# A decode block on one core: w_gate loaded first, its product and GELU ahead of q, the constants ahead of the statistics

## The chip, the core and the metric

The kernel runs on one core of a Trainium2 chip. The metric is the device time of one execution in microseconds (us). One execution was also recorded by the hardware profiler; its rows are what this document reads.

## The reference

One decode step for eight tokens. x (8 × 512) is normalised; attention over the last 1024 positions of a k and a v cache (32 query heads, 8 key heads, 128 wide) gives s; a GELU-gated feed-forward (512 to 1792 to 512) of the same normalised x gives g.

```
xn = layernorm(x)
q = xn @ wq                                   # 8 x 4096
s = softmax(q k^T / sqrt(128)) v @ wo         # window: last 1024 of 4096 positions
g = silu((gelu(xn @ w_gate) * (xn @ w_up)) @ w_down)
out = x + s * g
```

All tensors are bf16. The core reads 47.46 MB: 32 MiB of caches, 4 MiB each of wq and wo, and 1.75 MiB each of w_gate, w_up and w_down.

## The kernel before

The order of work on every engine is the program order; the kernel schedules it by hand. All large loads are issued by SP into one DMA queue, in this order: wq, k of batches 0 and 1, v of batch 0, then in the batch loop k of batch b+2 and v of batch b+1, and after the loop w_gate, w_up, w_down and wo. Each k or v of a batch is two loads of 1 MiB. x goes in five small pieces through ScalarE's queue (L78).

SBUF has eight slots of 16 KB per partition. `slot` (L66) hands them out in turn; two of the eight lie where wq lies, so the first loads that take these two (k of batch 3, v of batch 2) wait until the q product is done. A load into a used slot waits for the last reader of what lay there. Each DMA also waits for the eighth one before it, whose semaphore it takes over.

The front: VectorE (DVE) writes a few constants, waits for x, computes mean and variance (L137, L139), ScalarE the root (L141), and x normalised is transposed by TensorE (PE) into xnR (L159 to L161). Then the q product (L254) fills eight PSUM banks with 32 matmuls. Behind the statistics DVE and GpSimd (POOL) write the masks and selectors (neg_st, neg_mv, sel, own, pick, oT) and DVE clears qbd (L245), a block-diagonal copy of q. q is cast to bf16, transposed and copied into qbd (L264 to L277).

The loop: for each batch `turn_k` (L242) transposes k on DVE, `scores` (L304) multiplies it by qbd, `softmax` (L312) takes maximum and exponent, `turn_p` (L337) transposes the weights, `values` (L348) multiplies by v, and `gather` and `regroup` (L369 to L400) put the heads where the wo product wants them.

The tail: products of xnR with w_gate (z_ps) and w_up (u_ps) at L459, GELU of z by the tanh form (L469 to L477), the product with u (L479), a transpose (L482), the product with w_down (f_ps, L488), silu (L496 to L500), the product with wo (s_ps, L507) in four parts as wo lands, two DVE steps (L515, L517) and the store (L519).

Of the kernel before, what the change touches and what calls it, by code (L numbers as in the profile page):

```python
# [7 lines left out]
ACT = mybir.ActivationFunctionType  # L8
ALU = mybir.AluOpType
AX = mybir.AxisListType  # L10
BF16 = mybir.dt.bfloat16
FP32 = mybir.dt.float32
I32 = mybir.dt.int32
PSUM = bass.MemoryType.PSUM

N_SLOTS = 8
RB = 4
# [4 lines left out]
def kernel(  # L22
# [13 lines left out]
    nc = tc.nc  # L36

    B, Sq, D = A_x.shape
    Hkv, Sk, Dh = A_k_cache.shape[1], A_k_cache.shape[2], A_k_cache.shape[3]
    Hq = A_wq.shape[1] // Dh  # L40
# [3 lines left out]
    F = B_w_gate.shape[1]  # L44
    inv = float(Dh) ** -0.5
    P = nc.NUM_PARTITIONS
    NK = D // P
    HG = 4
    NG = Hkv // HG
    C = W * HG // P  # L50
    ROW = C * Dh
    FT = F // 4
    NJ = F // P
    DT = D // 4
# [3 lines left out]
    keep = ctx.enter_context(tc.tile_pool(name="keep", bufs=1))  # L58
# [7 lines left out]
    def slot(name):  # L66
        i = taken[0] % N_SLOTS
        taken[0] += 1
        if i >= 2:
            return ring.tile([P, 2 * ROW], BF16, name=name, tag="slot")  # L70
        if not late:
            late.append(ctx.enter_context(tc.tile_pool(name="late", bufs=2)))
        return late[0].tile([P, 2 * ROW], BF16, name=name, tag="slot")


    x_sb = keep.tile([B, D], BF16, name="x_sb")
# [19 lines left out]
    def load_v(b):  # L96
        v_sb[b] = load_cache(A_v_cache, b, "v_sb")

    wq_v = A_wq.rearrange("(p k) n -> p k n", k=NK)
    wq_all = wq_pool.tile([P, NK, Hq * Dh], BF16, name="wq_sb")  # L100
    nc.sync.dma_start(out=wq_all, in_=wq_v)
    wq_sb = [wq_all[:, k, :] for k in range(NK)]
# [5 lines left out]
    ident = consts.tile([P, P], BF16, name="ident")  # L108
    nc.vector.memset(ident, 0.0)
    nc.gpsimd.affine_select(  # L110
        out=ident,
        in_=ident,
# [6 lines left out]
    eps_sb = consts.tile([B, 1], FP32, name="eps_sb")  # L119
    nc.vector.memset(eps_sb, 1e-5)  # L120
    xnR = keep.tile([P, NK, 4, 32], BF16, name="xnR")
    nc.vector.memset(xnR, 0.0)
    xpad = keep.tile([B, 32], BF16, name="xpad")
    nc.gpsimd.memset(xpad, 0.0)
    nc.gpsimd.affine_select(
        out=xpad,
        in_=xpad,
# [3 lines left out]
        pattern=[[-1, 32]],  # L131
        channel_multiplier=RB,
    )


    stats = keep.tile([B, nc.vector.BN_STATS_DIM], FP32, name="stats")
    nc.vector.bn_stats(out=stats, in_=x_sb)  # L137
    mv = keep.tile([B, nc.vector.BN_AGGR_DIM], FP32, name="mv")
    nc.vector.bn_aggr(out=mv, in_=stats)  # L139
    rstd = keep.tile([B, 1], FP32, name="rstd")  # L140
    nc.scalar.activation(out=rstd, in_=mv[:, 1:2], func=ACT.Sqrt, bias=eps_sb, scale=1.0)  # L141
    nc.vector.reciprocal(out=rstd, in_=rstd)
    xhat = keep.tile([B, D], BF16, name="xhat")
    nc.vector.tensor_scalar(  # L144
        out=xhat,
        in0=x_sb,
        scalar1=mv[:, 0:1],
        scalar2=rstd[:, 0:1],
        op0=ALU.subtract,
        op1=ALU.mult,  # L150
    )
    x_res = keep.tile([P, DT], FP32, name="x_res")
    warm = keep.tile([B, 1], FP32, name="warm")
    nc.scalar.activation(out=warm, in_=rstd, func=ACT.Exp)  # L154
    with tc.tile_pool(name="ps_x", bufs=1, space=PSUM) as ps_x:
        xnT_ps = ps_x.tile([P, NK, B], BF16, name="xnT_ps")
        xv = xhat.rearrange("b (p k) -> b k p", k=NK)
        for k in range(NK):
            nc.tensor.transpose(xnT_ps[:, k, :], xv[:, k, :], ident[0:B, 0:B])  # L159
        for j in range(4):  # L160
            nc.vector.tensor_copy(out=xnR[:, :, j, 0 : RB * B : RB], in_=xnT_ps)  # L161
        xr_ps = ps_x.tile([P, DT], FP32, name="xr_ps")
        for t in range(4):
            nc.tensor.matmul(
                xr_ps[32 * t : 32 * t + 32, :],
                xpad,
                x_sb[:, t * DT : (t + 1) * DT],
                start=True,
                stop=True,
            )  # L170
        nc.scalar.copy(out=x_res, in_=xr_ps)  # L171

    qd = Hq // NG
# [6 lines left out]
        out=hv,  # L182
        in_=hv,
# [7 lines left out]
        out=neg_st,  # L191
        in_=neg_st,
# [8 lines left out]
        out=neg_mv,  # L201
        in_=neg_mv,
# [5 lines left out]
    )  # L208

    NU = Hq // 8
    sel = consts.tile([P, NG, Hq], FP32, name="sel")
    nc.vector.memset(sel, 0.0)
    for g in range(NG):
        nc.vector.tensor_reduce(
            out=sel[:, g, g * qd : (g + 1) * qd],
            in_=ident.rearrange("p (t g h) -> p g h t", t=4, g=NG)[:, g],
            axis=AX.X,
            op=ALU.add,  # L220
# [3 lines left out]
        out=own, in_=ident.rearrange("p (i e) -> p e i", e=8), axis=AX.X, op=ALU.add  # L224
    )
    pick = consts.tile([P, 4 * NU], BF16, name="pick")
    with nc.allow_low_precision(reason="sums of zeros and a single one"):
        nc.vector.tensor_reduce(
            out=pick, in_=ident.rearrange("p (a e) -> p a e", e=8), axis=AX.X, op=ALU.add
# [2 lines left out]
    nc.vector.memset(oT, 0.0)  # L232

    qbd = keep.tile([P, 2, B, 2, NG, 4 * Hq], BF16, name="qbd")
    kT = {}

    def turn_k(b, g):  # L240
        t = kT_pool.tile([P, ROW], BF16, name="kT")
        nc.vector.transpose(out=t.bitcast(I32), in_=k_sb[b][:, g].bitcast(I32))  # L242
        kT[b, g] = t

    nc.vector.memset(qbd, 0.0)  # L245
    turn_k(0, 0)
    q_both = slot("q_both")
    q_bf = q_both[:, 0:ROW]
# [1 line left out]
    with tc.tile_pool(name="ps_q", bufs=1, space=PSUM) as ps_q:  # L250
        q_ps = [ps_q.tile([P, 512], FP32, name=f"q_ps{i}") for i in range(8)]
        for k in range(NK):
            for i in range(8):
# [4 lines left out]
                    start=(k == 0),  # L258
                    stop=(k == NK - 1),
# [165 lines left out]
            regroup(0)  # L425


    wgu = []
    for w in (B_w_gate, B_w_up):
        tv = slot("wgu_sb")[:, 0 : NK * F].rearrange("p (k f) -> p k f", k=NK)  # L430
        nc.sync.dma_start(out=tv, in_=w.rearrange("(p k) f -> p k f", k=NK))
        wgu.append(tv)
    wd = slot("wd_sb")[:, 0 : NJ * D].rearrange("p (j d) -> p j d", d=D)
    nc.sync.dma_start(out=wd, in_=B_w_down.rearrange("(p j) d -> p j d", j=NJ))
    wo = []
    for u in range(NU):
        if u % 2 == 0:
            pair = slot("wo_sb").rearrange("p (v j d) -> p v j d", v=2, d=D)
        t = pair[:, u % 2]
# [11 lines left out]

    ps_f = ctx.enter_context(tc.tile_pool(name="ps_f", bufs=1, space=PSUM))
    ffn = ctx.enter_context(tc.tile_pool(name="ffn", bufs=1))
    zu = []
    for n, ws in (("z_ps", wgu[0]), ("u_ps", wgu[1])):
        ps = ps_f.tile([P, FT], FP32, name=n)
        for k in range(NK):
            for t in range(4):
                nc.tensor.matmul(  # L459
                    ps[32 * t : 32 * t + 32, :],  # L460
                    xnR[:, k, t, :],
                    ws[:, k, t * FT : (t + 1) * FT],
                    start=(k == 0),
                    stop=(k == NK - 1),
                )
        zu.append(ps)
    z_ps, u_ps = zu
    z2 = ffn.tile([P, FT], FP32, name="z2")
    nc.scalar.activation(out=z2, in_=z_ps, func=ACT.Square)  # L469
    nc.vector.tensor_scalar(  # L470
        out=z2, in0=z2, scalar1=0.044715, scalar2=1.0, op0=ALU.mult, op1=ALU.add
    )
    nc.vector.tensor_tensor(out=z2, in0=z2, in1=z_ps, op=ALU.mult)
    th = ffn.tile([P, FT], FP32, name="th")
    nc.scalar.activation(out=th, in_=z2, func=ACT.Tanh, scale=0.7978845608028654)
    nc.vector.tensor_scalar(out=th, in0=th, scalar1=0.5, scalar2=0.5, op0=ALU.mult, op1=ALU.add)
    nc.vector.tensor_tensor(out=th, in0=th, in1=z_ps, op=ALU.mult)  # L477
    h_bf = ffn.tile([P, FT], BF16, name="h_bf")
    nc.vector.tensor_tensor(out=h_bf, in0=th, in1=u_ps, op=ALU.mult)  # L479

    hT = ffn.tile([P, NJ, 32], BF16, name="hT")
    nc.vector.transpose(  # L482
        out=hT.rearrange("p j b -> p (j b)"), in_=h_bf.rearrange("p (y j) -> p j y", j=NJ)
    )
    f_ps = ps_f.tile([P, DT], FP32, name="f_ps")
    for j in range(NJ):
        for t in range(4):
# [4 lines left out]
                start=(j == 0),  # L492
                stop=(j == NJ - 1),
# [4 lines left out]
        out=g_sb, in0=g_sb, scalar1=0.5, scalar2=0.5, op0=ALU.mult, op1=ALU.add  # L498
# [5 lines left out]
    for u in range(NU):  # L504
        for j in range(8):
            for t in range(4):
# [4 lines left out]
                    start=(u == 0 and j == 0),  # L511
                    stop=(u == NU - 1 and j == 7),
# [7 lines left out]
        out=out_f.rearrange("b (t d) -> t b d", t=4), in_=out_sb[0 : P : RB, :]  # L520
# [31 lines left out]
```

## Time and profile before

| | |
|---|---|
| median of 3 runs (lowest to highest) | 121.13 us (120.96 to 121.29) |
| the profiled execution | 121.08 us |
| its span | 119.2 us |
| busy: PE, DVE, ACT, POOL | 70.9, 75.7, 31.4, 3.2 us |
| mean rate of the DMA engines | 399 GB/s |
| share of DMA in the chain that ended last | 78% |

The span runs from the first instruction to the last; 1.86 us of the profiled execution lie around it. In the rows of slices a digit is the busy share of a fortieth of the span, in tenths. In the chain that ended last each piece is what released the next. In a timeline a row has its start in us, its duration, the engine, the line, the operation and its tiles; in a list of waits the numbers are the total in us, how often, and the longest. SPq is SP's instruction queue, in which a load's issue stands until its waits are met.

### The profile page before, as it was taken

Reading aid. Unit: us, or ns where it says so; the run is one execution under the profiler, and the core shown is the slowest. Engines: PE = TensorE matmul, PEld = TensorE weight load, DVE = VectorE, ACT = ScalarE, POOL = GpSimd, SP = SyncE. Lnnn points to the kernel's source line nnn. Section 1 sums busy time; section 2 is a strip of 40 time slices with the busy share of each in tenths; the row PEclk is TensorE's granted clock in tenths of the full one; section 3 lists DMA queues with packets and bytes.
Section 4 is the critical chain, followed back from the end, with each engine's and each line's share of the span. In section 5 each row is a group of like instructions: output and inputs, shape, how many; then the busy total and the mean of one; then the engine's idle time right before and its main releaser. Section 6 shows DMA issues by size and latency. Waiting matters only on the chain.

```text
span 119.2 us, 2306 instructions
## 1 busy us (share of the span) xinstructions
PE 70.9 (59%) x992; PEld 37.9 (32%) x992; DVE 75.7 (63%) x101; ACT 31.4 (26%) x75; POOL 3.2 (3%) x10
## 2 busy tenths in 40 slices
PE   0000079971299498896969692875783547544370
PEld 0000033420034154453635451433452433143350
DVE  1000387969998999999999968949952241751000
ACT  0300240076500715144161700421618101100000
POOL 2000052000000000000000000000000000000000
PEclk9999999998559999999999999999999755555555
DMA  6898899999999999999999999999999999999930
GB/s 177 352 518 363 374 429 432 423 429 426 434 418 423 434 426 421 426 432 418 423 432 426 421 423 429 423 429 421 423 429 433 443 438 404 438 414 429 402 140 3
DMA packets 6110, 47.61 MB, mean 399 GB/s; under 512 B 716, under 2 KB 852, under 8 KB 1108
## 3 DMA queue, kind: packets, MB, share of 16 engines
q1 hardware_dynamic: 6084, 47.46, 94.7%
q8 instruction: 8, 0.13, 0.4%
q14 instruction: 2, 0.02, 0.0%
q10 hardware_dynamic: 16, 0.01, 0.0%
HBM read 47.46 MB, written 0.01 MB: 398 GB/s over the span
## 4 chain that ended last, share of the span: by engine, by line
DMA 78%; PE 9%; DVE 6%; ACT 2%; issue 1%; ACTq 1%; DVEq 0%; SPq 0%
DMA k_sb<-in_A_k_cache_dram 32%; DMA wo_sb<-in_A_wo_dram 20%; DMA v_sb<-in_A_v_cache_dram 16%; DMA x_sb<-in_A_x_dram 9%; PE q_ps L254 8%; DVE qbd L277 3%; ACTq L78 1%; DVE q_both L267 1%; ACT L154 1%; DVE q_both L264 1%; PE s_ps L507 1%; DVE stats L137 1%; DVE y L515 0%; ACT rstd L141 0%; DVE out_sb L517 0%
## 5 line engine op out<-in xcount | busy, mean ns | idle before, releaser
L304 PE MATMUL S_ps<-kT,qbd 128*128 128x512 bf16 x128 | 31.9, 393 | 14.8 <-DVE kT L242 11.3
L242 DVE STREAM_TRANSPOSE kT<-k_sb 128x2048 int32<-128x2048 int32 x16 | 36.5, 2286 | 1.6 <-DMA k_sb<-in_A_k_cache_dram 1.6
L304 PEld LDWEIGHTS <-qbd 128*128 128x128 bf16 x128 | 12.6, 99 | 30.8 <-issue 14.2
L324 ACT ACTIVATE nb<-m 32x1 f32<-32x1 f32 x32 | 6.4, 201 | 20.1 <-DVE m L321 19.8
L326 ACT ACTIVATE P_sb<-S_ps,nb 128x1024 bf16<-128x1024 f32 x8 | 11.1, 1390 | 0.3
L348 PE MATMUL O_ps<-v_sb,pT 128*32 128x128 bf16 x512 | 9.2, 227 | 2.6 <-DVE pT L337 2.6
L314 DVE TENSOR_REDUCE mx<-S_ps 128x1 f32<-128x1024 f32 x8 | 9.6, 1194 | 1.6 <-PE S_ps L304 1.6
L254 PE MATMUL q_ps<-wq_sb,xnR 128*128 128x512 bf16 x32 | 9.9, 485 | 0.5 <-ACT x_res L171 0.5
L348 PEld LDWEIGHTS <-pT 128*32 128x32 bf16 x512 | 7.7, 100 | 5.6 <-issue 3.0
L159 PE MATMUL xnT_ps<-ident,xhat 8*128 8x8 bf16 x4 | 0.3, 174 | 15.2 <-DVE xhat L144 15.2
L361 ACT COPY O_sb<-O_ps 128x256 f32<-128x256 f32 x8 | 3.0, 372 | 22.7 <-PE O_ps L348 22.7
L137 DVE BATCH_NORM_STATS2 stats<-x_sb 8x6 f32<-8x512 bf16 x1 | 0.7, 681 | 12.0 <-DMA x_sb<-in_A_x_dram 12.0
L337 DVE STREAM_TRANSPOSE pT<-P_sb 128x512 int32<-128x512 int32 x8 | 5.7, 711 | 3.4 <-ACT P_sb L326 3.3
L507 PE MATMUL s_ps<-wo_sb,oT 128*32 128x128 bf16 x128 | 4.4, 307 | 3.9 <-DMA wo_sb<-in_A_wo_dram 3.9
L369 PE MATMUL o_ps<-O_sb,sel 128*32 128x128 f32 x32 | 5.4, 297 | 0.9 <-ACT O_sb L361 0.9
L293 PE MATMUL S_ps<-neg_mv,neg_st 128*128 128x512 bf16 x16 | 4.8, 381 | 1.9 <-DVE q_both L264 1.9
L254 PEld LDWEIGHTS <-xnR 128*128 128x128 bf16 x32 | 3.8, 118 | 6.4 <-issue 3.9
L264 ACT CAST q_both<-q_ps 128x512 bf16<-128x512 f32 x6 | 3.0, 613 | 8.6 <-PE q_ps L254 8.6
L507 PEld LDWEIGHTS <-oT 128*32 128x32 bf16 x128 | 3.5, 136 | 4.9 <-issue 4.7
L159 PEld LDWEIGHTS <-xhat 8*128 8x128 bf16 x4 | 0.2, 113 | 15.2 <-DVE xhat L144 15.2
L515 DVE TENSOR_TENSOR y<-s_ps,g_sb 128x128 f32<-128x128 f32 x1 | 0.3, 292 | 7.4 <-PE s_ps L507 7.4
L369 PEld LDWEIGHTS o_ps<-O_sb,sel 128*32 128x32 f32 x32 | 3.0, 115 | 4.0 <-issue 2.5
(64 smaller groups left out, 53.9 us busy)
## 6 DMA issues: line engine op xcount, KB each, us to landing
k_sb<-in_A_k_cache_dram SPq DMA_DIRECT2D x16, 1024.0 KB, 16.5
v_sb<-in_A_v_cache_dram SPq DMA_DIRECT2D x16, 1024.0 KB, 19.8
wq_sb<-in_A_wq_dram SPq DMA_DIRECT2D x1, 4096.0 KB, 12.2
wo_sb<-in_A_wo_dram SPq DMA_DIRECT2D x3, 1024.0 KB, 25.0
wgu_sb<-in_B_w_gate_dram SPq DMA_DIRECT2D x1, 1792.0 KB, 21.3
wgu_sb<-in_B_w_up_dram SPq DMA_DIRECT2D x1, 1792.0 KB
wd_sb<-in_B_w_down_dram SPq DMA_DIRECT2D x1, 1792.0 KB
wo_sb<-in_A_wo_dram SPq DMA_DIRECT2D x1, 640.0 KB
```

What stands on the lines that cost most here:

```text
L242: nc.vector.transpose(out=t.bitcast(I32), in_=k_sb[b][:, g].bitcast(I32))
L254: nc.tensor.matmul(q_ps[i], xnR[:, k, :, :].rearrange("p j b -> p (j b)"), wq_sb[k][:, i * 512 : (i + 1) * 512], start=(k == 0), stop=(k = ...
L264: e(out=q_bf[:, i * 512 : (i + 1) * 512], in_=q_ps[i])
L293: nc.tensor.matmul(S[b][:, half, :], neg_st.rearrange("p j h -> p (j h)"), neg_mv.rearrange("p a n -> p (a n)"), start=True, stop=False,)
L304: nc.tensor.matmul(S[b][:, half, :], qbd[:, m, b, w, g, :], kv[:, half * 16 : (half + 1) * 16, m, :, w], start=False, stop=(g == NG - 1 an ...
L314: nc.vector.tensor_reduce(out=mx, in_=S[b].rearrange("p a c -> p (a c)"), axis=AX.X, op=ALU.max)
L324: nc.scalar.mul(nb[32 * j : 32 * j + 32, :], m1, -inv)
L326: nc.scalar.activation(out=P_sb[b].rearrange("p c i w -> p c w i"), in_=S[b].rearrange("p a (c w i) -> p (a c) w i", w=2, i=32), func=ACT.Exp,
L337: nc.vector.transpose(out=pT[b].rearrange("p c h w -> p (c h w)").bitcast(I32), in_=P_sb[b].rearrange("p c i w -> p (c i w)").bitcast(I32),)
L348: nc.tensor.matmul(O_ps[b][32 * t : 32 * t + 32, g, :], pT[b][:, c // 2, :, c % 2], vv[:, c, :], start=(c < 4), stop=(c >= C - 4),)
L369: nc.tensor.matmul(o[:, 0:Dh], sel[:, g, :], O_sb[b][:, g, :], start=(g == 0), stop=(g == NG - 1))
L507: nc.tensor.matmul(s_ps[32 * t : 32 * t + 32, :], oT[:, j, u, :], wo[u][:, j, t * DT : (t + 1) * DT], start=(u == 0 and j == 0), stop=(u = ...
```

## The change

w_gate becomes the first load of SP's queue, ahead of wq. Its slot is the first of the eight, so the slots of later tiles move on by one: v of batch 1 and k of batch 3 now take the two that lie on wq. The masks and selectors, and the clearing of qbd, move ahead of x's statistics on DVE and POOL. The product with w_gate is placed ahead of the q product on PE, in a PSUM pool of its own (`ps_z`) that is closed before q's pool opens, and the GELU is placed ahead of the first `turn_k` on DVE and ahead of q's casts on ScalarE; its result is kept in a new tile, gz. After the loop only w_up is loaded and multiplied, and h_bf is gz times u_ps. The arithmetic is the same.

```diff
+    def load_ffn(w):
+        t = slot("wgu_sb")[:, 0 : NK * F].rearrange("p (k f) -> p k f", k=NK)
+        nc.sync.dma_start(out=t, in_=w.rearrange("(p k) f -> p k f", k=NK))
+        return t
+
+    wg_sb = load_ffn(B_w_gate)
     wq_all = wq_pool.tile([P, NK, Hq * Dh], BF16, name="wq_sb")
     nc.sync.dma_start(out=wq_all, in_=wq_v)
...
+    (neg_st, neg_mv, sel, own, pick, oT and the clearing of qbd, unchanged, from below)
     stats = keep.tile([B, nc.vector.BN_STATS_DIM], FP32, name="stats")
     nc.vector.bn_stats(out=stats, in_=x_sb)
...
+    gz = keep.tile([P, 512], FP32, name="gz")[:, 0:FT]
...
+    def project(ps, ws):
+        for k in range(NK):
+            for t in range(4):
+                nc.tensor.matmul(ps[32 * t : 32 * t + 32, :], xnR[:, k, t, :],
+                    ws[:, k, t * FT : (t + 1) * FT], start=(k == 0), stop=(k == NK - 1))
+
+    zctx = ExitStack()
+    ps_z = zctx.enter_context(tc.tile_pool(name="ps_z", bufs=1, space=PSUM))
+    z_ps = ps_z.tile([P, FT], FP32, name="z_ps")
+    project(z_ps, wg_sb)
...
-    nc.vector.memset(qbd, 0.0)
+    with tc.tile_pool(name="gelu", bufs=1) as gelu:
+        (the six GELU steps, unchanged, from below; the last writes gz)
+    zctx.close()
     turn_k(0, 0)
...
-    wgu = []
-    for w in (B_w_gate, B_w_up):
-        ...
+    wu_sb = load_ffn(B_w_up)
...
-    zu = []
-    for n, ws in (("z_ps", wgu[0]), ("u_ps", wgu[1])):
-        ...
-    (the six GELU steps)
+    u_ps = ps_f.tile([P, FT], FP32, name="u_ps")
+    project(u_ps, wu_sb)
     h_bf = ffn.tile([P, FT], BF16, name="h_bf")
-    nc.vector.tensor_tensor(out=h_bf, in0=th, in1=u_ps, op=ALU.mult)
+    nc.vector.tensor_tensor(out=h_bf, in0=gz, in1=u_ps, op=ALU.mult)
```

More of the change, by code (lines that the diff above doesn't have):

```diff
@@ L133 @@
     )
[L136 to L171, printed above, removed]
     qd = Hq // NG
@@ L237 @@
     qbd = keep.tile([P, 2, B, 2, NG, 4 * Hq], BF16, name="qbd")
+    nc.vector.memset(qbd, 0.0)
+    stats = keep.tile([B, nc.vector.BN_STATS_DIM], FP32, name="stats")
+    nc.vector.bn_stats(out=stats, in_=x_sb)
+    mv = keep.tile([B, nc.vector.BN_AGGR_DIM], FP32, name="mv")
+    nc.vector.bn_aggr(out=mv, in_=stats)
+    rstd = keep.tile([B, 1], FP32, name="rstd")
+    nc.scalar.activation(out=rstd, in_=mv[:, 1:2], func=ACT.Sqrt, bias=eps_sb, scale=1.0)
+    nc.vector.reciprocal(out=rstd, in_=rstd)
+    xhat = keep.tile([B, D], BF16, name="xhat")
+    nc.vector.tensor_scalar(
+        out=xhat,
+        in0=x_sb,
+        scalar1=mv[:, 0:1],
+        scalar2=rstd[:, 0:1],
+        op0=ALU.subtract,
+        op1=ALU.mult,
+    )
+    x_res = keep.tile([P, DT], FP32, name="x_res")
+    gz = keep.tile([P, 512], FP32, name="gz")[:, 0:FT]
+    warm = keep.tile([B, 1], FP32, name="warm")
+    nc.scalar.activation(out=warm, in_=rstd, func=ACT.Exp)
+    with tc.tile_pool(name="ps_x", bufs=1, space=PSUM) as ps_x:
+        xnT_ps = ps_x.tile([P, NK, B], BF16, name="xnT_ps")
+        xv = xhat.rearrange("b (p k) -> b k p", k=NK)
+        for k in range(NK):
+            nc.tensor.transpose(xnT_ps[:, k, :], xv[:, k, :], ident[0:B, 0:B])
+        for j in range(4):
+            nc.vector.tensor_copy(out=xnR[:, :, j, 0 : RB * B : RB], in_=xnT_ps)
+        xr_ps = ps_x.tile([P, DT], FP32, name="xr_ps")
+        for t in range(4):
+            nc.tensor.matmul(
+                xr_ps[32 * t : 32 * t + 32, :],
+                xpad,
+                x_sb[:, t * DT : (t + 1) * DT],
+                start=True,
+                stop=True,
+            )
+        nc.scalar.copy(out=x_res, in_=xr_ps)
+    def project(ps, ws):
+        for k in range(NK):
+            for t in range(4):
+                nc.tensor.matmul(
+                    ps[32 * t : 32 * t + 32, :],
+                    xnR[:, k, t, :],
+                    ws[:, k, t * FT : (t + 1) * FT],
+                    start=(k == 0),
+                    stop=(k == NK - 1),
+                )
+    zctx = ExitStack()
+    ps_z = zctx.enter_context(tc.tile_pool(name="ps_z", bufs=1, space=PSUM))
+    z_ps = ps_z.tile([P, FT], FP32, name="z_ps")
+    project(z_ps, wg_sb)
     kT = {}
@@ L243, in turn_k @@
         kT[b, g] = t
-    nc.vector.memset(qbd, 0.0)
+    with tc.tile_pool(name="gelu", bufs=1) as gelu:
+        z2 = gelu.tile([P, FT], FP32, name="z2")
+        nc.scalar.activation(out=z2, in_=z_ps, func=ACT.Square)
+        nc.vector.tensor_scalar(
+            out=z2, in0=z2, scalar1=0.044715, scalar2=1.0, op0=ALU.mult, op1=ALU.add
+        )
+        nc.vector.tensor_tensor(out=z2, in0=z2, in1=z_ps, op=ALU.mult)
+        th = gelu.tile([P, FT], FP32, name="th")
+        nc.scalar.activation(out=th, in_=z2, func=ACT.Tanh, scale=0.7978845608028654)
+        nc.vector.tensor_scalar(
+            out=th, in0=th, scalar1=0.5, scalar2=0.5, op0=ALU.mult, op1=ALU.add
+        )
+        nc.vector.tensor_tensor(out=gz, in0=th, in1=z_ps, op=ALU.mult)
+    zctx.close()
     turn_k(0, 0)
@@ L425 @@
             regroup(0)
-    wgu = []
-    for w in (B_w_gate, B_w_up):
-        tv = slot("wgu_sb")[:, 0 : NK * F].rearrange("p (k f) -> p k f", k=NK)
-        nc.sync.dma_start(out=tv, in_=w.rearrange("(p k) f -> p k f", k=NK))
-        wgu.append(tv)
+    wu_sb = load_ffn(B_w_up)
     wd = slot("wd_sb")[:, 0 : NJ * D].rearrange("p (j d) -> p j d", d=D)
@@ L453 @@
     ffn = ctx.enter_context(tc.tile_pool(name="ffn", bufs=1))
-    zu = []
-    for n, ws in (("z_ps", wgu[0]), ("u_ps", wgu[1])):
[L456 to L477, printed above, removed]
+    u_ps = ps_f.tile([P, FT], FP32, name="u_ps")
+    project(u_ps, wu_sb)
     h_bf = ffn.tile([P, FT], BF16, name="h_bf")
-    nc.vector.tensor_tensor(out=h_bf, in0=th, in1=u_ps, op=ALU.mult)
+    nc.vector.tensor_tensor(out=h_bf, in0=gz, in1=u_ps, op=ALU.mult)
     hT = ffn.tile([P, NJ, 32], BF16, name="hT")
```

## The prediction

> **What bounds the kernel now.** I read the page's rows of DMA share first, then the chain that ended last, then the waits of the DMA queue and of the engines, and last the two ends of the timeline.
>
> The span in 40 slices of 2.98 us, and the queues:
>
> ```profile
> DMA  6898899999999999999999999999999999999930
> GB/s 177 352 518 363 374 429 432 423 429 426 434 418 423 434 426 421 426 432 418 423 432 426 421 423 429 423 429 421 423 429 433 443 438 404 438 414 429 402 140 3
> ...
> q1 hardware_dynamic: 6084, 47.46, 94.7%
> ```
>
> From the sixth slice to the 38th the 16 DMA engines never rest, whatever the compute engines do. The uneven slices before come from 32 KB packets counted where they start: in the packet records of the trace all 16 engines are at work from 2.9 us to 113.5 us, at 425 to 434 GB/s but for a few dips to 412 where code is fetched. 47.46 MB at 428 GB/s is 110.9 us of a span of 119.2.
>
> The end of the chain, and the tail of the timeline:
>
> ```profile
> 90.48 0.02 issue
> 90.49 24.12 DMA wo_sb<-in_A_wo_dram
> 114.62 0.04 issue
> 114.66 1.25 PE s_ps L507 x27
> ```
>
> ```profile
> PE s_ps L507 <- DMA wo_sb<-in_A_wo_dram: 3.9, 4, 1.5
> SPq L83 <- DMA wq_sb<-in_A_wq_dram: 9.8, 1, 9.8
> SPq L83 <- PE q_ps L254: 5.7, 1, 5.7
> ```
>
> The last product (L507) waits for each of four pieces of wo; so the end is set by the last bytes, plus 3.7 us of product, two DVE steps and the store. SP's queue waits for q_ps too, but by then it has more than ten us of loads ahead of it, so that wait costs nothing.
>
> The front, where the change works:
>
> ```profile
> 2.53 10.64 DMA x_sb<-in_A_x_dram
> ```
>
> ```profile
> 16.22 9.94 PE L254 MATMUL q_ps<-wq_sb,xnR 128*128 128x512 bf16 x32 [0.52 <-ACT x_res L171]
> ...
> 18.85 3.47 DVE L245 MEMSET qbd<- 128x4096 uint32 x1 [0.80 <-issue]
> ...
> 26.19 1.18 SPq L83 DMA_DIRECT2D k_sb<-in_A_k_cache_dram  x2
> ```
>
> x, 8 KB in five pieces, lands whole only at 13.17 us, just behind wq; the q product ends at 26.16 and lets SP issue the load that takes wq's place in SBUF.
>
> **The change, part by part.** The sum is made against the profiled execution: 121.08 us, its span 119.2 and 1.86 around it; the median of the runs shown is 121.13.
>
> Bytes: the same loads, none added, none removed; w_gate's 1.75 MiB stand first instead of after v. A MiB takes 2.44 us (landings of k's halves: 15.44, 17.88, 20.21). So every load from wq to the last v lands 1.75 × 2.44 = 4.28 us later, and w_up, w_down and wo land where they did. Cost on the stream: 0, if it never runs dry.
>
> Start of the stream: wq's first 16 packets took 1.80 us on average against 1.21 for the later ones, 0.59 lost. They end together at 3.75 to 4.2 us however early they began (1.83 to 2.69), which looks like one common event: then smaller packets lose the same. If the loss grew with packet size, w_gate's 14,336 B against 32,768 would lose 0.26, a gain of 0.33. I take -0.1, nearer the first.
>
> x: after its first piece (landed about 2.4 us) its pieces landed at 7.90, 10.40, 12.80 and 13.17, one 32 KB packet (1.21 us) passing between any two of x's steps on the engine that carries it. Behind w_gate the packets are of 0.535 us (rows of w_gate at 93 us) and the engine has eight; w_gate lands at 2.7 + 8 × 0.535 = 7.0 us, and x's last piece has one or two wq packets to sit out after that: 8.4 us, by my estimate; bounds 5.5 (nothing to wait for) and 17.5 (x behind wq as well).
>
> The constants: 0.17 + 0.27 + 0.11 + 0.42 + 0.37 + 0.28 + 0.48 + 3.47 = 5.57 us of DVE plus its gap of 0.80, from 1.32 to about 7.7. Ahead of the statistics they are covered by DVE's wait for x (12.0 us in the profile). If x came at 5.5 they would delay it by 2.2 us, still without cost, since q must wait for wq. POOL's three selects (0.58, 0.29, 1.56) move with them and feed nothing before L293.
>
> z and GELU: from x's landing to the first product took 13.17 to 16.22, 3.05 us; z takes 1.68 (98.92 to 100.60, at half clock), the GELU behind it 3.51 (to 104.11: two ScalarE and four VectorE steps with their hand-overs). So 8.4 + 3.05 + 1.68 + 3.51 = 16.6 us. The new order makes q's first weight load wait for the last GELU step on DVE and for ScalarE, because z's PSUM is handed on to q. Behind that wait are queued all of q, then the scores. wq lands at 13.02 + 4.28 = 17.3, so the wait for z is covered by 0.7 us and q starts at about 17.4, against 16.22. It ends 9.94 later at 27.3, against 26.16: 1.1 us later.
>
> Who waits for that: SP's issue of v of batch 1, which takes wq's place, and every load behind it. Ahead of it are w_gate, wq, k of 0, 1 and 2 and v of 0, 13.75 MiB, which drain at 13.02 + 9.75 × 2.44 = 36.8 us. With 1.0 us from issue to first packet (0.81 to 1.83) the issue must come by 35.8. Margin 8.5 us. Later waits for buffers keep what they had: data is 4.28 us later, compute 1.1.
>
> The middle: DVE's 7 us per batch against 9.8 us of loads per batch catches up either way.
>
> The tail: v of batch 7 lands about 97.1 instead of 92.8, and its value product (93.41 to 95.05) moves by 3.7 us; the regrouping ends at 103.2 instead of 99.46. w_up's product then runs 102.7 to 104.4, and with the GELU done one multiply (0.62) and the transpose (0.98) follow, so f_ps starts at 106.1 against 105.90 and ends at 107.9; w_down has landed at 105.7. The first wo lands at 108.1 as before. So 3.5 us of GELU leave the tail, 3.7 us of late data take the place, and neither shows, since L507 has until 111.9 to start (four pieces of 1.04 and the last bytes at 115.55). Saved at the end: 0.
>
> Sum: 121.08 - 0.1 = 121.0 us.
>
> On PE's clock: the q product issued every 0.43 us until 22.1 and every 0.21 after, so a start from rest runs at half rate for some 6 us. Worst, all 32 at 0.43 make 13.7 us, and q would end at 31.1, still 4.7 us before the stream needs it. The Trainium skill, TensorE: Matmul & The Clock Gate, in the section on the HAM clock gate, says that some 3.4 us of sustained work are needed for the full clock and that an idle window of that length takes it back. By it z's 1.7 us burst and the 3.5 us rest for the GELU warm nothing, and q runs as it did; the trace has no short burst followed by such a rest at the front to test this.
>
> **The rivals.**
>
> Faster: the end of the stream is ragged. The last load's 16 parts land from 113.70 to 115.55; engines that carried a 16 KB code fetch (0.88 to 0.97 us each, seven up to 110 us) finish last. If the moved instructions shift these fetches so that the worst engine is hit less, up to 0.5 us goes, and with the 0.33 of the start 0.2 to 0.8: 120.6. For it: the PE's code has another order. Against it: the same 1882 PE instructions, so as many fetches.
>
> Slower, by the same thing: one engine is hit by two 16 KB fetches. The latest then ends another 0.9 to 1.5 us later: 122.2. It decides as soon as two fall on one engine; so far nine fetches lag nine different engines, which speaks against it.
>
> Slower, by x: x lands only behind wq, at 17.5 us. Then z and GELU are no longer covered: q starts at 17.5 + 3.05 + 1.68 + 3.51 = 25.7 and ends at 35.7, right at the 35.8 from which the stream runs dry; each us beyond costs one. With all of q at half rate it ends at 39.5, 3.7 late. Between 0 and 3.7 I take 1.8: 122.9. For it: x landed with wq in the profile. Against it: its pieces came one packet apart, not in a block. The Trainium skill, DMA: Bandwidth & Descriptors, under Queues, rings and completion order, has an engine take some 9 to 17 descriptors from one queue before it turns to the other; w_gate and wq together are 16 per engine, so by that rule x would come behind both. The trace disagrees: one 32 KB packet between turns, 1.21 us.
>
> That the change doesn't do what it says (GELU still in the tail) is excluded by the program order; it would give no change too.
>
> **How the numbers follow.** About 0.3% (0.36 us) is what a measurement of this kernel can tell from no change. No change (120.8 to 121.5): 0.58. Faster by the ragged end or the start: 0.24, at 120.6. Slower: two fetches on one engine 0.10, x behind wq 0.05, a crowded tail or a wait that I do not see 0.03: together 0.18. The range takes the forecast's own, the faster case down to 120.4 and the near half of the slower cases, to 121.9.
>
> **What would show it.** Right: GB/s of 420 or more from slice 6 to 38 and a first wo landing near 108; x landed at 7 to 10 us, the last GELU step before 17.5, q from about 17.4 to 27.3; SP's v of batch 1 issued near 27 with no dip at 37 us; L507 still idle for wo. Wrong: a slice under 400 GB/s near 37 us (x late), the last load's landings spread over more than 2.5 us or less than 1.5 (code fetches), or L507 starting after 111.9 us.

## The result: 0.3% slower, by the slowest of 16 DMA engines

The changed kernel takes 121.53 us (median of 7 runs, 121.48 to 121.65), the kernel before, run beside it, 121.17 (7 runs, 120.96 to 121.38). The ratio is 1.0029, with a 95% interval of 1.0018 to 1.0041. That is inside the range that was given, and about the 0.3% named as the least that counts, but it is a loss that the interval sets apart from zero, where no change or a tenth of a microsecond gained was forecast. The profiled execution took 121.56 us, with a span of 119.8 (before 121.08 and 119.2). The span grew by more than the time: by 0.62 us in the profiled executions, of which 0.15 came back because less time lies around the span (1.71 us, before 1.86; over all runs some 1.74 and 1.87). What sets that part no run here shows, so the experiments below are compared by when their last bytes land as well as by their times.

The page's rows of the DMA engines and the main queue, of the changed kernel (40 slices of 3.0 us):

```profile
DMA  5899999999999999999999999999999999999920
GB/s 116 374 454 471 394 399 429 429 418 435 429 427 421 424 432 429 416 427 432 418 427 418 435 421 424 429 427 424 427 421 427 434 436 441 409 421 427 385 84 3
...
q1 hardware_dynamic: 6084, 47.46, 94.4%
```

```profile
SPq L83 <- PE q_ps L287: 9.0, 1, 9.0
```

There is no dip anywhere near 37 us: the stream was never dry, and SP's longer wait for q (9.0 us against 5.7) cost nothing. The end of the chain that ended last, and PE's waits:

```profile
92.23 23.00 DMA wo_sb<-in_A_wo_dram
115.23 0.04 issue
115.28 1.26 PE s_ps L514 x30
```

```profile
PE s_ps L514 <- DMA wo_sb<-in_A_wo_dram: 4.6, 4, 2.2
```

The last part of the wo product (L514, before L507) starts at 115.28 instead of 114.66. The longest wait for wo has grown from 1.5 to 2.2 us. The two middle parts of that product show where, first in the timeline of before, then in that of the changed kernel (start, duration, and in brackets the idle time in front):

```profile
110.62 1.04 PE L507 MATMUL s_ps<-wo_sb,oT 128*32 128x128 bf16 x32 [1.41 <-DMA wo_sb<-in_A_wo_dram]
113.11 1.05 PE L507 MATMUL s_ps<-wo_sb,oT 128*32 128x128 bf16 x32 [1.45 <-DMA wo_sb<-in_A_wo_dram]
```

```profile
110.56 1.04 PE L514 MATMUL s_ps<-wo_sb,oT 128*32 128x128 bf16 x32 [1.41 <-DMA wo_sb<-in_A_wo_dram]
113.77 1.04 PE L514 MATMUL s_ps<-wo_sb,oT 128*32 128x128 bf16 x32 [2.17 <-DMA wo_sb<-in_A_wo_dram]
```

Up to the second wo load the two kernels are level; the third comes 0.66 us later, and the lateness stays. The packet records of the trace say why. Every load is cut into 16 equal parts, one for each DMA engine, and the load has landed when its last part has. How far the last part lies behind the first is called the spread here:

| load | before: first part, spread | changed: first part, spread |
|---|---|---|
| the first of all (wq; w_gate) | 12.52, 0.50 | 6.91, 1.31 |
| wq | 12.52, 0.50 | 16.63, 1.27 |
| the second of wo | 108.70, 1.87 | 108.59, 1.93 |
| the third of wo | 111.20, 1.87 | 111.03, 2.69 |
| the last piece of wo | 113.69, 1.85 | 113.58, 2.60 |

The first part of the last piece is even 0.1 us earlier than before; its last part, at 116.18 instead of 115.55, is 0.63 later. Three engines leave w_gate 1.17, 1.18 and 1.31 us behind the first one and stay there to within about 0.1 us, load after load. A fetch of 16 KB of code, whose packet takes 0.9 us on one engine, puts that engine some 1.5 us back for good (before, at 45.97: from 0.35 to 1.85; changed, at 47.53: from about 0.5 to 2.07). The fetches are of PE's code: with most of it left out (e10 below) two are left of eight. As long as the fetches fall on engines that are level, the spread stays near 1.9. In the changed kernel the fetch at 109.72 falls on an engine that has lain 1.1 us back since w_gate: 2.69.

The Trainium skill, DMA: Bandwidth & Descriptors, in the section on why a DMA increments its semaphore by 16, says that the engines of one DMA finish independently and that only the full count means that all has landed. The trace agrees, with 16 landings of one load up to 2.69 us apart.

### The profile page after: what moved, and what is told of

It is laid out like the page before. It is cut to its first block, busy times and chain, and to the rows that moved or that the text cites. A ratio compares the mean times of both kernels' runs of the same rounds, so it can differ in the third digit from the quotient of the medians.

```text
span 119.8 us, 2299 instructions
## 1 busy us (share of the span) xinstructions
PE 68.0 (57%) x985; PEld 37.0 (31%) x992; DVE 75.9 (63%) x101; ACT 31.4 (26%) x75; POOL 3.1 (3%) x10
## 4 chain that ended last, share of the span: by engine, by line
DMA 94%; SPq 1%; PE 1%; DVE 0%; issue 0%
DMA v_sb<-in_A_v_cache_dram 68%; DMA wo_sb<-in_A_wo_dram 19%; DMA wgu_sb<-in_B_w_gate_dram 6%; SPq L83 1%; PE s_ps L514 1%; DVE y L522 0%; DVE out_sb L524 0%
## 5 line engine op out<-in xcount | busy, mean ns | idle before, releaser
L337 PE MATMUL S_ps<-kT,qbd 128*128 128x512 bf16 x128 | 31.4, 389 | 16.9 <-DVE kT L262 13.3
L287 PE MATMUL q_ps<-wq_sb,xnR 128*128 128x512 bf16 x31 | 8.8, 449 | 3.6 <-DVE gz L277 3.5
L381 PE MATMUL O_ps<-v_sb,pT 128*32 128x128 bf16 x512 | 8.6, 220 | 2.6 <-DVE pT L370 2.6
L381 PEld LDWEIGHTS <-pT 128*32 128x32 bf16 x512 | 7.2, 97 | 5.6 <-issue 3.0
L514 PE MATMUL s_ps<-wo_sb,oT 128*32 128x128 bf16 x128 | 4.4, 307 | 4.6 <-DMA wo_sb<-in_A_wo_dram 4.6
L514 PEld LDWEIGHTS <-oT 128*32 128x32 bf16 x128 | 3.5, 136 | 5.6 <-issue 5.4
L297 DVE CAST q_both<-q_ps 128x512 bf16<-128x512 f32 x2 | 1.3, 672 | 5.9 <-PE q_ps L287 5.9
L326 PE MATMUL S_ps<-neg_mv,neg_st 128*128 128x512 bf16 x10 | 3.5, 383 | 1.8 <-DVE q_both L297 1.8
## 6 DMA issues: line engine op xcount, KB each, us to landing
wq_sb<-in_A_wq_dram SPq DMA_DIRECT2D x1, 4096.0 KB, 16.6
```

The costliest lines, as they stand in the source:

```text
L287: nc.tensor.matmul(q_ps[i], xnR[:, k, :, :].rearrange("p j b -> p (j b)"), wq_sb[k][:, i * 512 : (i + 1) * 512], start=(k == 0), stop=(k = ...
L297: e(out=q_bf[:, i * 512 : (i + 1) * 512], in_=q_ps[i])
L326: nc.tensor.matmul(S[b][:, half, :], neg_st.rearrange("p j h -> p (j h)"), neg_mv.rearrange("p a n -> p (a n)"), start=True, stop=False,)
L337: nc.tensor.matmul(S[b][:, half, :], qbd[:, m, b, w, g, :], kv[:, half * 16 : (half + 1) * 16, m, :, w], start=False, stop=(g == NG - 1 an ...
L381: nc.tensor.matmul(O_ps[b][32 * t : 32 * t + 32, g, :], pT[b][:, c // 2, :, c % 2], vv[:, c, :], start=(c < 4), stop=(c >= C - 4),)
L514: nc.tensor.matmul(s_ps[32 * t : 32 * t + 32, :], oT[:, j, u, :], wo[u][:, j, t * DT : (t + 1) * DT], start=(u == 0 and j == 0), stop=(u = ...
```

## The experiments

The theory drawn from these rows: **ragged start**. With w_gate as the first load the 16 engines leave the start unevenly; the lag never goes, and with a code fetch on top it sets the end. Rivals: **moved code** (PE's new order puts two fetches on one engine, whatever the start) and **crowded tail** (late data push the last products). What each run gave, with the spread of the first load and of the last piece of wo, and when that piece's last part landed:

| kernel | first spread | last spread | last byte | ratio to before (95%) |
|---|---|---|---|---|
| before | 0.50 | 1.85 | 115.55 | |
| changed | 1.31 | 2.60 | 116.18 | 1.0029 (1.0018 to 1.0041) |
| e11 changed, again | 1.16 | 2.47 | 116.02 | 1.0022 (1.0012 to 1.0031) |
| e1 wq first | 0.56 | 1.94 | 115.69 | 1.0003 (0.9994 to 1.0011) |
| e2 w_gate's load alone | 1.26 | 2.53 | 116.18 | 1.0051 (1.0033 to 1.0068) |
| e3 wq in four pieces | 0.37 | 1.84 | 115.50 | 1.0015 (1.0003 to 1.0027) |
| e4 one fetch less | 1.03 | 2.38 | 115.88 | 1.0034 (1.0021 to 1.0047) |
| e5 wq, 14 KB rows first | 0.46 | 2.00 | 115.68 | 1.0029 (1.0017 to 1.0042) |
| e6 w_up first | 1.44 | 1.83 | 115.59 | 1.0007 (0.9996 to 1.0019) |
| e7 w_gate alone, x behind | 1.39 | 1.81 | 115.69 | 1.0067 (1.0048 to 1.0086) |
| e8, e12 half of k first | 0.80, 0.81 | 1.90, 1.85 | 115.77, 115.67 | 0.9989 (0.9980 to 0.9998), 0.9999 (0.9989 to 1.0008) |
| e9 an extra read of wq | 1.34 | 2.79 | 120.60 | one run, 126.4 us |
| e10 little code | 1.02 | 1.78 | 115.36 | 0.9980 (0.9955 to 1.0004) |

**e1: the order of two loads undone.**

```diff
-    wg_sb = load_ffn(B_w_gate)
     wq_all = wq_pool.tile([P, NK, Hq * Dh], BF16, name="wq_sb")
     nc.sync.dma_start(out=wq_all, in_=wq_v)
     wq_sb = [wq_all[:, k, :] for k in range(NK)]
+    wg_sb = load_ffn(B_w_gate)
```

> The changed kernel with one line moved: wq is loaded first and w_gate second; all else as changed. Ragged start (my theory): with 14 KB rows first the 16 DMA engines come out of their first load 1.3 us apart instead of 0.5, keep that lag since every load is cut evenly over them, and the last code fetch (at 109.7 us) then hits a lagging one. So here the parts of the first load land within 0.6 us of each other, those of the last within 1.9, and the time is that of the kernel before (ratio 0.999 to 1.001), though q ends some 5 us later. Moved code (rival): the order of PE's instructions puts two code fetches on one engine; that order is unchanged here, so the last spread stays 2.6 us and the ratio 1.003. Crowded tail (rival): compute is later still, so 1.003 or more.

Ragged start holds to the tenth: first spread 0.56, last 1.94, ratio 1.0003. All the rest of the change is still in it, and later than ever, as its timeline shows:

```profile
17.45 1.68 PE L245 MATMUL z_ps<-wgu_sb,xnR 128*32 128x448 bf16 x16 [1.72 <-DMA wgu_sb<-in_B_w_gate_dram]
22.67 9.99 PE L287 MATMUL q_ps<-wq_sb,xnR 128*128 128x512 bf16 x32 [3.54 <-DVE gz L277]
```

q ends at 32.7 us, 6.5 later than before, and costs nothing. The product, the GELU, the constants and the new order of PE's code are worth zero; the loss came with the place of one load. Moved code and crowded tail fall. The times of the fetches shift too (the last one that meets data starts at 111.35 instead of 109.72), but no engine lay more than 0.56 us back at the start for one to fall on.

**e2: that load alone.** Into a tile of its own; z and th take over qbd's space at the end.

```diff
+    wg_own = keep.tile([P, NK, F], BF16, name="wgu_sb")
+    nc.sync.dma_start(out=wg_own, in_=B_w_gate.rearrange("(p k) f -> p k f", k=NK))
     wq_all = wq_pool.tile([P, NK, Hq * Dh], BF16, name="wq_sb")
...
+    wgu.append(wg_own)
-    for w in (B_w_gate, B_w_up):
+    for w in (B_w_up,):
...
```

> The kernel before with only the load of w_gate moved to the front, into a tile of its own; z, GELU and the constants stay where they were. Ragged start: first load's parts 1.3 us apart; if the last code fetch goes to the same engine as in the changed kernel, last spread 2.6 us and ratio 1.003, and anyhow a first spread over 1 us. Moved code: PE's code is that of before, so last spread 1.85 and ratio 1.000. Crowded tail: GELU is in the tail and v lands 4.3 us later, so it would be slower than the changed kernel, over 1.004.

The spreads came as ragged start has it (1.26, 2.53), with PE's code as before, so moved code falls here too. The ratio, 1.0051, is the one that a crowded tail was to give (over 1.004), and PE is late, with the GELU still in the tail:

```profile
112.76 3.71 PE L511 MATMUL s_ps<-wo_sb,oT 128*32 128x128 bf16 x128
```

The wo product starts at 112.76, later than the 111.9 that the prediction gave as the limit, and the row shows no gap. But a row merges matmuls whose ends are modelled, and the end of the chain that ended last tells more:

```profile
97.80 18.39 DMA wo_sb<-in_A_wo_dram
116.18 0.04 issue
116.22 0.27 PE s_ps L511 x4
```

PE had caught up: its last four matmuls still waited for the last bytes, and start at 116.22 as in the changed kernel. So the data set the end here, and the limit of 111.9 was too strict. The spans of e2 (119.8 us on average) are those of the changed kernel; one of its ten runs, of 122.59 us, pulls the ratio up, and the other nine average 121.59. That the GELU had to leave the tail this run does not show; e6 and e7 below, with the same late tail, lose 0.27 and 0.84 us in it in another way.

**e3 and e5: is it the length of the rows?** Both load wq in pieces in the kernel before.

```diff
-    nc.sync.dma_start(out=wq_all, in_=wq_v)
+    for k in range(NK):                                   # e3: rows of 8 KB
+        nc.sync.dma_start(out=wq_all[:, k], in_=wq_v[:, k])
```

> The kernel before with wq loaded in four pieces of 1 MiB, so that its rows are 8 KB instead of 32 KB; nothing else. Ragged start by row size: the first piece's parts land 1.3 us apart or more and all later ones too; the time is the same or up to 0.5% longer, by what the code fetches hit. Ragged start by something else in w_gate (its place in memory, or the load behind it): spread 0.5 us as before, ratio 1.000. Moved code and crowded tail: ratio 1.000, spread 0.5.

```diff
-    nc.sync.dma_start(out=wq_all, in_=wq_v)
+    wq_o = wq_all.rearrange("p k n -> p (k n)")
+    wq_i = A_wq.rearrange("(p k) n -> p (k n)", k=NK)
+    for c0, c1 in ((0, 7168), (7168, NK * Hq * Dh)):      # e5: first 14,336 B of 32 KB
+        nc.sync.dma_start(out=wq_o[:, c0:c1], in_=wq_i[:, c0:c1])
```

> The kernel before with wq loaded in two pieces: of each partition's 32 KB the first 14,336 B, then the rest. So the first load has rows of w_gate's length, but they start 32 KB apart in wq. Row length theory: first spread over 1 us. Place theory (what counts is where the engines' reads begin in memory: w_gate's rows start 14,336 B apart and each engine's share 112 KiB apart, no power of two): first spread 0.3 to 0.6 us as with wq whole, last spread at most 1.95, time 120.9 to 121.4.

Row length falls twice: first spreads of 0.37 and 0.46. The times do not go with it: both are slower than before though their last bytes land at 115.50 and 115.68. In their profiled executions (121.53 and 121.49 us, before 121.08) 1.14 and 0.99 us of the span lie behind the landing of the store, against 0.83 before, and 2.05 and 1.98 us lie around the span, against 1.86; the store itself lands 0.05 earlier in e3 and 0.13 later in e5. That is the whole difference: 0.45 and 0.41 us. So what these two lose, they lose in the main behind the work; why, with more loads, stays open.

**e6, e7 and e9: w_gate's address, x, or how far its rows lie apart?** w_gate's rows start 14,336 B apart; those of wq start 32 KB apart.

```diff
-    wg_own ... in_=B_w_gate.rearrange("(p k) f -> p k f", k=NK)
+    wg_own ... in_=B_w_up.rearrange("(p k) f -> p k f", k=NK)       # e6, against e2
...
```

> As e2, but w_up takes w_gate's place as the first load (the same shape in another tensor), and w_gate is loaded late. Place theory by shape, and row length theory: first spread 1.0 to 1.3 us and time 121.3 to 121.8. If it is w_gate's own address alone: spread near 0.5 and 121.1.

```diff
-    for r, z in ((0, 2), (2, 4), (4, 6), (6, 7), (7, 8)):           # e7, against e2
-        nc.scalar.dma_start(out=x_sb[r:z], in_=A_x.flatten_outer_dims()[r:z])
...
     nc.sync.dma_start(out=wq_all, in_=wq_v)
+    for r, z in ((0, 2), (2, 4), (4, 6), (6, 7), (7, 8)):
+        nc.sync.dma_start(out=x_sb[r:z], in_=A_x.flatten_outer_dims()[r:z])
```

> As e2 (w_gate's load first, the rest as before), with x's five small loads issued by SP behind wq instead of by ScalarE beside it. Theory that x's small packets, coming in between w_gate's first rows, push engines apart: first spread 0.5 us. Place or row length theory: first spread still 1.0 to 1.3 us. x lands near 17.5 us and q ends near 30 us, which by every theory costs the stream nothing; time 121.3 to 121.8 by the last two, 121.1 by the first.

```diff
+    nc.sync.dma_start(                                              # e9, against before
+        out=qbd.rearrange("p a b c d e -> p (a b c d e)")[:, 0 : NK * F],
+        in_=A_wq.rearrange("a b -> (a b)")[0 : P * NK * F].rearrange("(p f) -> p f", p=P),
+    )
     wq_all = wq_pool.tile([P, NK, Hq * Dh], BF16, name="wq_sb")
```

> The kernel before with one load more ahead of all: the first 1.75 MiB of wq read as 128 rows of 14,336 B, one behind the other (w_gate's shape, in wq's memory), into qbd, which is then cleared as before. 4.3 us longer than before by its bytes, about 125.4 us; what counts is the first spread. If the distance of the rows makes the engines start unevenly: 1.0 us or more, as with w_gate. If it is the tensor's own place in memory: 0.5 us, as with wq.

w_up has the lag too (1.44), without x's packets it stays (1.39), and wq's own memory, read in rows 14,336 B apart, has it (1.34). The pages' rows of issues give the same, from issue to the landing of the slowest part, for 1792 KB as the first load: e9, then e5.

```profile
qbd<-in_A_wq_dram SPq DMA_DIRECT2D x1, 1792.0 KB, 7.5
```

```profile
wq_sb<-in_A_wq_dram SPq DMA_DIRECT2D x1, 1792.0 KB, 6.7
```

Same tensor, same amount, same row length; what differs is the distance of the rows in memory (and the tile that they are written to), and the slowest engine is 0.8 us later. It begins with the first packet of each engine: these 16 end within 0.47 us of each other in wq (3.75 to 4.22) and 0.48 in e5, but 1.35 us apart in e9 and 1.66 in the changed kernel. Why that distance starts the engines unevenly no run here shows. e9's time is 1.0 us over the 125.4 that its bytes alone gave, 0.8 of it by its last byte.

In e6 one engine alone lagged (1.44; the next 0.51), no code fetch fell on it, and the last byte came at 115.59: the lag alone costs nothing, being less than what one fetch costs any engine. In e7 a fetch fell on an engine 0.78 back (2.29), and at 88.0 another fell on the engine that led, so that the spread, which counts from the first part, shrank to 1.81; its last byte came at 115.69. Both times miss what was expected (121.3 to 121.8): e6 with 121.25, e7 with 122.0 (two runs), the worst of the kernels without an extra load. e7's tail in the timeline:

```profile
115.40 0.29 PE L511 MATMUL s_ps<-wo_sb,oT 128*32 128x128 bf16 x6 [0.16 <-DMA wo_sb<-in_A_wo_dram]
116.53 0.29 PE L511 MATMUL s_ps<-wo_sb,oT 128*32 128x128 bf16 x6 [0.84 <-issue]
```

PE stands idle for 0.84 us ahead of its last six matmuls and waits for nothing that the profile shows; a code fetch ran from 114.23 to 115.16, and they start 1.37 us behind its end. In e6 the fetch ended at 114.55, and the same six start 1.32 us behind it, after 0.27 us idle. In the changed kernel no fetch starts between 109.72 and 116.25, and its last matmul starts at 116.23. That PE waited for its code is likely, but was not tested.

**e4 and e10: the code fetches.**

```diff
-            for c in range(C):
+            Cb = C // 2 if b < 4 else C      # e4; in e10 Cb = 4
+            for c in range(Cb):
...
```

> The changed kernel without the second half of each head group's positions in the value product of batches 0 to 3 (128 matmuls and 128 weight loads fewer, their v is still loaded): PE's code is one fetch of 16 KB shorter, so the fetch that came at 109.7 us should fall behind the last load. Ragged start plus that fetch: first spread 1.3 us as in the changed kernel, last spread 1.9 to 2.0 instead of 2.6, end 0.6 us earlier, ratio to before 0.996 to 0.999. If the fetch has no part in it (front lag alone, or the tail): ratio 1.003 as for the changed kernel.

> The changed kernel with most of PE's code left out (value products of 4 instead of 32 positions per head group, a quarter of the score products, 2 of 8 parts of each wo product, 2 of 14 of w_down's): 498 instructions instead of 1882, the same loads. At most one code fetch is left before the end. Front lag plus code fetches: first spread 1.0 to 1.3 us as in the changed kernel, last spread no more than 1.6, last byte at 115.2 or before instead of 116.18, time about 120.3 (ratio 0.990 to 0.996). If the front lag alone, or something else in the stream, makes the end late: last spread over 2 us and ratio 1.000 or more.

e4 missed: the fetch still came at 110.2 us, and another one, at 47.9, had already fallen on an engine that lay 1.0 back (1.03 to 2.51). Last spread 2.38, ratio 1.0034 where 0.996 to 0.999 was expected. So it is not one fetch in particular; one that falls on a lagging engine does it. e10 leaves two fetches, by its page and its tail:

```profile
q8 instruction: 2, 0.03, 0.1%
```

```profile
115.41 0.30 PE L515 MATMUL s_ps<-wo_sb,oT 128*32 128x128 bf16 x4 [0.62 <-DMA wo_sb<-in_A_wo_dram]
```

With w_gate still first (1.02) the last spread is 1.78 and the last byte 0.8 us earlier than in the changed kernel. The direction is as expected, the size less (1.6 and 115.2 were); its times scatter from 120.4 to 121.6 and show a gain against the changed kernel, not one against before.

**e8 and e12: a less uneven start for the changed kernel.** Half of batch 0's k goes ahead of w_gate.

```diff
...
+    load_half(0)                 # k of batch 0, first 1 MiB
     wg_sb = load_ffn(B_w_gate)
     wq_all = wq_pool.tile([P, NK, Hq * Dh], BF16, name="wq_sb")
...
-    load_k(0)
+    load_half(1)
```

> The changed kernel with the first half of batch 0's k (1 MiB, 8 KB rows) loaded ahead of w_gate; all else as changed. If the raggedness arises only from which load comes first, the first load's parts land within 0.5 us as with wq in 8 KB pieces, w_gate's then also within 0.5, the last within 1.9, and the ratio to before is 0.999 to 1.001. If any load of w_gate makes the engines uneven, wherever it stands: w_gate's parts land 1 us or more apart and the ratio stays near 1.003.

> e8 once more (the changed kernel with half of batch 0's k ahead of w_gate), to see whether its gain over the kernel before holds. Front lag theory: first spread under 1 us on all engines but one, last spread 1.9 to 2.0, ratio 0.998 to 1.000. If e8's ratio was an accident: 1.000 to 1.002.

In e8 one engine lags by 0.80, the others by 0.51 at most, and w_gate as the second load adds little (0.94); in e12 two lag, by 0.74 and 0.81. The last spread is that of before, and so is the time; the 0.1% of e8 did not come back in e12. The start is less uneven, not even: no fetch fell on these engines, and whether one would have is chance as far as these traces go. e11, the changed kernel once more, gave its lag and its loss again:

> The changed kernel once more, as the mark for the run beside it. Front lag as a property of the load: first spread again 1.0 to 1.4 us, last spread 2.3 to 2.7, ratio 1.002 to 1.004. If the lag was an accident of one execution: first spread anywhere from 0.4, ratio 1.000 to 1.004.

Over all profiled executions but e9's: of the seven with rows 14,336 B apart first, four have their last byte at 115.88 to 116.18 (changed, e11, e2, e4); of the other three, e10 has little code, and in e6 and e7 the fetches fell luckily. All six with another first load, the kernel before among them, have it at 115.50 to 115.77. So the uneven start makes a late end possible, and where the fetches fall decides.

## Why the prediction was right or wrong

**The bound: right.** The last bytes set the end in both kernels, with all 16 engines at work throughout.

**"Cost on the stream: 0, if it never runs dry": the step that failed.** It never ran dry, and its last bytes came 0.63 us later all the same (0.36 us in the medians of the times). The sum took the engines for one pipe of 428 GB/s. Each load waits for the slowest engine, and in these traces an engine's lag of a microsecond stays, to within 0.1 or 0.2, to the end. That 121.53 us lies inside the range is luck: the range reached there for rivals that did not come.

**"Start of the stream", -0.1: the term that was mis-sized.** It asked what the first 16 packets lost on average (0.59 us of wq's, 0.60 of w_gate's: no difference, as far as that goes) and took the common end of wq's for a property of the start. It was one of wq's rows. What counted was the worst engine, 0.96 us lost against 1.70, and how far apart the first packets end, 0.47 us against 1.66. The gain of 0.1 is not there: the first part of the last piece lands 0.1 us earlier, but the load ends with its last part.

**The ragged end: right place, wrong cause.** The prediction saw that the last load's parts lie 1.85 us apart and that code fetches do it, and asked whether two would fall on one engine. None did. A fetch fell on an engine late from the start, and the prediction had not put the two lags together.

**The front: wrong in size, without cost.**

```profile
12.31 0.68 DVE L205 BATCH_NORM_STATS2 stats<-x_sb 8x6 f32<-8x512 bf16 x1 [4.67 <-DMA x_sb<-in_A_x_dram]
...
19.78 0.62 DVE L277 TENSOR_TENSOR gz<-th,z_ps 128x448 f32<-128x448 f32 x1
...
20.46 8.89 PE L287 MATMUL q_ps<-wq_sb,xnR 128*128 128x512 bf16 x31 [3.55 <-DVE gz L277]
...
29.39 1.18 SPq L83 DMA_DIRECT2D v_sb<-in_A_v_cache_dram  x2
```

x landed at 12.2 us, not 8.4: its last two pieces each let two wq packets of 1.21 us pass, one ahead of the data and one ahead of the signal, where one or two in all were counted. So the GELU ended at 20.4 instead of 16.6, and q at 29.4 instead of 27.3, with 6.4 us to spare of the 8.5. q itself took 8.9 us, not 9.94: by the granted clock its half rate ended 3.7 us after its start, not 5.8 as before. In e11, the same kernel, it was 2.9 us, in e1 5.9, so it differs from one execution to the next. z's 1.69, the GELU's 3.5 and the constants under the wait for x came as worked out. On the rule of 9 to 17 descriptors between turns (the Trainium skill, DMA: Bandwidth & Descriptors, Queues, rings and completion order) the trace again disagrees: one packet of 1.21 us.

**The tail: right.** f_ps began at 105.85 (forecast 106.1, before 105.90), and the wo product waited for each of its loads.

## What to carry to other kernels

Where a kernel is bound by its loads, work out the end for the slowest DMA engine, not for their sum: look at how far the 16 landings of a load lie apart, from the first load on. Put a load with evenly starting rows first (here rows 32 KB apart: 0.4 to 0.6 us), and the odd one second. Moving work out of a tail that waits for data gains nothing (e1), and the order of two loads that the sum calls free can lose 0.3%.

## What was not expected of the hardware

But for the code fetches, the first load decides how even the engines are to the end: 0.4 to 0.6 us apart with wq first, 1.0 to 1.4 with rows that start 14,336 B apart, in all three tensors tried. A fetch of 16 KB of code, 0.9 us by its packet, puts its engine 1.5 us back: PE's code comes through the same engines as the data.
